# A fused attention and feed-forward block: features scaled in place of weights, four query tiles finished early, and the projection's rest in row-split runs

## The chip, the cores and the metric

The kernel runs on one core of a Trainium2 chip, as one program. The metric is the device time of one execution in microseconds (us). The engines are TensorE (PE; its weight loads are PEld), VectorE (DVE), ScalarE (ACT), GpSimd (POOL) and SyncE (SP). Each works through its own queue in order, and semaphores tie the queues together. SP does nothing but issue transfers; a transfer that waits for its data holds up those issued behind it.

## What is computed

One transformer block on x, 2048 tokens (S) by 576 features (D), with 32 heads of 18 and a hidden layer of 4608, all in bf16:

```
sa, ca, ga, sb, cb, gb = silu(c) @ w_mod          # six rows of 576
h  = layernorm(x) * (1 + ca) + sa
q, k, v = h @ wqkv                                # 32 heads of 18
phi(y) = [softmax(y @ w_phi), softmax(-y @ w_phi)]
o  = (phi(q) @ (phi(k).T @ v)) / (phi(q) @ sum(phi(k)) + 1e-6)
x  = x + ga * (o @ wo)
h  = layernorm(x) * (1 + cb) + sb
x  = x + gb * (relu(h @ w1) @ w2)
```

## The kernel before

The tokens are 16 tiles of 128. The work has a head, which an order written out by hand sets, and then eight blocks of the feed-forward, two tiles each.

**The head.** ORDER is a string of words; a loop (L671) calls a job for each, so every engine gets its instructions in that order. A number after a colon is the pair of PSUM banks that the job writes. The jobs:
- `sc`, `sh` (L251): the two modulation rows of the first norm, with matmuls on zeros between (`Z` are such matmuls alone, L235). `ca` (L509) makes ca1 = 1 + ca, one value per feature and so one per partition.
- `FK` (L442) and `FQ` (L259): w_phi folded into the weights of k and q, in five chunks of 116 features. Each chunk leaves PSUM twice: scaled by ca1 into wk or wq (`fs` L451, `fsd` L448, `fsr` L623, `FQs` L636) and unscaled into wfold (`fra`, `frd` L455 and L457, `frr` L625, `FQra`, `FQrd` L515 and L517). `wsd` (L524) scales the five chunks of the weights of v.
- `KR`, `VR` (L268), `KRh` (L482), `KRd` (L486): four constant rows from the unscaled weights, put into the fifth chunk at rows 96 to 99. `QR`, `QRh`, `QRe`, `QRd` do it for q, by four small transfers.
- `bn` (L240, L241), `sa` (L588 to L590), `sp` (L594 to L596): mean and deviation of each token; `T`, `Tc` (L582, L585) turn them into rows 96 to 99 of the turned features xT. Mean and shift thus come out of the matmul, and 1/deviation is the exponential's scale.
- `K`, `V`, `Q` (L274): the projections, ten matmuls for each tile; `Ka` and `Kb` are four chunks and the fifth. `eK`, `eQ` (L279): both exponentials. `sK` (L284) row sums, `rK` (L301, L302), `pA` (L599), `pM` (L603, L604, L291), `vE` (L305): the softmax factors; `kv` (L324) adds a tile to phi(k).T v in banks 6 and 7, from five buffers E_sb and four buffers v_sb.
- `sq`, `qi` (L336, L339): a query tile of exponentials goes to DRAM and back, since EQ holds six tiles (SLOT); tiles under QF = 2 stay on chip. `qs` (L284, L343), `qp` (L346, L291), `qt` (L350): their factors and the turned tile in ET, of four places.
- `m2`, `ga`, `gb`, `gaw`, `gar`: the other modulation rows; `wo` (L642) multiplies wo by ga on POOL. `wl`, `w2a`, `w2b`: the loads of w1 and w2 into the places of the earlier weights and of xT. `tp` (L479): differences of blocks of w2.
- `kz`, `nu` (L391), `nO` (L398, L399), `ot`, `oc`, `W` (L408, L410), `lb`, `lr`, `ap`, `xc`, `ht`, `hd`, `ha`: tiles 0 and 1 go through the rest of the attention and the second norm. `W` adds x by a matmul with an identity (L408).

**The blocks.** Block b takes tiles 2b and 2b + 1 through the feed-forward: the first layer in three groups (L688, and L695, whose 64-row halves run side by side), relu (L702 to L704), and the second layer (L748) by seven products of half size in 14 positions, with sums on DVE and POOL (L724, L756, L760, L733 to L735). Hooks put the attention of the next two tiles between: `q_next` (qs, qp, qt and a qi three tiles on), `attend` (nu, nO and a transpose by transfer, L403), the projection with wo, residual and norm (L415, L240, L418, L424, L403), and the scaling of h (L872), for which the next block waits. Blocks 0 and 1 do the projection whole in the second layer (wo_mm, L410); blocks 2 to 6 do the rest of 64 rows right behind L695 (wo_rest, L815) and the other 512 rows in the next step (wo_full, L821). Block 7 has no next tiles.

Of the kernel before, what the change touches and what calls it, by code (L numbers as in the profile page):

```python
# [982 lines left out]
```

## Time and profile before

| | |
|---|---|
| median of 5 runs (lowest to highest) | 391.55 us (390.61 to 391.59) |
| the profiled execution | 391.45 us |
| its span on the core | 389.7 us |
| TensorE clock granted | 1.00 |
| head: to the first matmul of block 0 | 93.38 us |
| block 7 begins | 351.65 us |
| DMA | 44.36 MB, mean 114 GB/s |
| sq and qi: transfers of 288 KB | 14 and 14 |

The span is the time between the first and the last instruction that the profile records; the execution's time is longer by 1.75 us. A row of the profile has the line of the kernel, the engine, the operation, what it writes and reads, a count, the busy time, and the mean duration of one in ns. Matmuls are pipelined: one of 288 columns is listed with 286 ns, but thirty in a row take 3.68 us. "Idle before" is the time that the engine stood still just before an instruction, with the instruction that ended it.

### The profile page before, as it was taken

The page shows a single profiled execution, that of the slowest core. Times are in us where ns is not written, and L with a number is a line of the kernel's source. Part 1 is how long each engine was busy: PE and PEld are TensorE (multiplying, and loading weights), DVE is VectorE, ACT ScalarE, POOL GpSimd, SP SyncE. Part 2 cuts the span into 40 slices and gives each one's busy share as a digit, 9 for nine tenths or more (in the row PEclk, how much of TensorE's full clock was granted, in tenths as well). Part 3 has the DMA queues.
Part 4 walks back from the last instruction along what each step waited for, and adds up shares of the span by engine and source line. Part 5 has one row for each costly group of instructions (what it writes and reads, how often), then busy time and mean ns, then how long its engine had stood idle before and what let it go on. Part 6 is the DMA issues. An engine that isn't in the chain of part 4 may idle for free.

```text
span 389.7 us, 8936 instructions
## 1 busy us (share of the span) xinstructions
PE 381.5 (98%) x3710; PEld 310.4 (80%) x3711; DVE 245.0 (63%) x462; ACT 157.7 (40%) x370; POOL 119.6 (31%) x193
## 2 busy tenths in 40 slices
PE   8999999999999999999999999999999999999995
PEld 4777888878887888778878788888888788788884
DVE  1989988954879748755674485468365735542333
ACT  2788779689531233123302430341144114302510
POOL 2164958731101511730061026004500440041023
PEclk9999999999999999999999999999999999999999
DMA  8999839686621252341124124300520223100000
GB/s 300 421 420 398 309 121 358 163 306 211 136 56 35 45 122 52 66 96 30 35 63 108 35 19 90 97 19 19 122 36 19 47 62 35 36 0 32 3 0 32
DMA packets 49515, 44.36 MB, mean 114 GB/s; under 512 B 39361, under 2 KB 42050, under 8 KB 48706
## 3 DMA queue, kind: packets, MB, share of 16 engines
q1 hardware_dynamic: 49186, 43.59, 38.2%
q8 instruction: 29, 0.48, 0.5%
q10 hardware_dynamic: 288, 0.19, 0.2%
q14 instruction: 12, 0.10, 0.1%
HBM read 27.97 MB, written 6.49 MB: 88 GB/s over the span
## 4 chain that ended last, share of the span: by engine, by line
PE 92%; DVE 3%; ACT 2%; DMA 1%; issue 1%; POOL 1%; POOLq 0%; SPq 0%; DVEq 0%; ACTq 0%
PE PS L688 33%; PE PS L748 30%; PE PS L274 14%; PE PS L695 5%; PE PS L821 3%; PE PS L410 2%; PE PS L391 2%; PE PS L324 1%; DMA R<-in_wsc_dram 1%; ACT RT L279 1%; DVE st L240 1%; PE PS L251 1%; DVE h L872 1%; PE PS L442 0%; POOL x_sb L735 0%
## 5 line engine op out<-in xcount | busy, mean ns | idle before, releaser
L688 PE MATMUL PS<-h,R 128*128 128x256 bf16 x1152 | 132.8, 273 | 0.3 <-DVE h L872 0.3
L688 PEld LDWEIGHTS <-R 128*128 128x128 bf16 x1152 | 110.9, 98 | 15.7 <-issue 2.5
L748 PEld LDWEIGHTS <-RH 128*128 128x128 f16 x846 | 82.8, 98 | 20.8
L734 POOL TENSOR_TENSOR yt<-yt,gb_row 128x288 f32<-128x288 f32 x23 | 23.0, 1002 | 192.1 <-DVE yt L733 192.1
L702 ACT ACTIVATE RH<-PS 128x256 f16<-128x256 f32 x72 | 27.5, 382 | 113.4 <-PE PS L695 98.4
L748 PE MATMUL PS<-R,RH 128*128 128x288 bf16 (+1 forms) x558 | 72.4, 286 | 0.0
L704 DVE SCALAR_TENSOR_TENSOR RH<-PS,RH 128x256 f16<-128x256 f32 x72 | 28.9, 413 | 65.6 <-ACT RH L702 65.6
L279 ACT ACTIVATE RT<-PS,rs 128x576 bf16<-128x576 f32 x64 | 42.9, 749 | 8.5 <-PE PS L274 8.3
L703 ACT ACTIVATE RH<-PS 128x512 f16<-128x512 f32 x72 | 42.9, 596 | 6.2 <-PE PS L688 5.2
L748 PE MATMUL PS<-RT,RH 128*128 128x288 f16 x288 | 37.9, 286 | 0.0
L752 ACT ACTIVATE RS<-PS 128x288 f32<-128x288 f32 x24 | 9.8, 410 | 67.8 <-PE PS L748 67.8
L274 PE MATMUL PS<-RH,R 116*128 116x288 bf16 x240 | 31.8, 286 | 0.5 <-ACT RH L636 0.5
L274 PE MATMUL PS<-RH,RT 116*128 116x288 bf16 x240 | 31.7, 286 | 0.0
L274 PEld LDWEIGHTS <-R 116*128 116x128 bf16 x240 | 22.9, 98 | 6.4 <-issue 0.7
L274 PEld LDWEIGHTS <-RT 116*128 116x128 bf16 x240 | 22.7, 98 | 5.5
L733 DVE TENSOR_TENSOR yt<-PS,RS 128x288 f32<-128x288 f32 x23 | 10.4, 452 | 26.2 <-PE PS L748 19.2
L240 DVE BATCH_NORM_STATS2 st<-x_sb 128x6 f32<-128x288 bf16 x60 | 24.2, 445 | 0.5
L735 POOL TENSOR_TENSOR x_sb<-yt,x_sb 128x288 bf16<-128x288 f32 x31 | 22.5, 730 | 2.4 <-DVE yt L731 0.6
L284 DVE TENSOR_REDUCE Rk<-RT 128x64 f32<-128x1152 bf16 x16 | 21.2, 1332 | 1.4 <-ACT RT L279 1.4
L284 DVE TENSOR_REDUCE Rq<-RT 128x64 f32<-128x1152 bf16 x16 | 21.5, 1343 | 0.0
L695 PE MATMUL PS<-h,R 64*128 64x256 bf16 x288 | 19.9, 271 | 0.0
L291 POOL TENSOR_TENSOR RT<-RT,ratq 128x576 bf16<-128x576 bf16 x16 | 19.0, 1190 | 1.3
(125 smaller groups left out, 418.7 us busy)
## 6 DMA issues: line engine op xcount, KB each, us to landing
R<-in_w1a_dram SPq DMA_DIRECT2D x4, 1152.0 KB
eqd<-RT SPq DMA_DIRECT2D x14, 288.0 KB, 4.5
RT<-eqd SPq DMA_DIRECT2D x14, 288.0 KB, 3.0
R<-in_w2a_dram SPq DMA_DIRECT2D x3, 864.0 KB, 10.2
R<-in_w2b_dram SPq DMA_DIRECT2D x2, 1296.0 KB, 10.9
out_dram<-x_sb SPq DMA_DIRECT2D x15, 144.0 KB, 1.7
RT<-in_xT_dram SPq DMA_DIRECT2D x2, 640.0 KB
x_sb<-in_xk_dram SPq DMA_DIRECT2D x3, 288.0 KB
```

Source lines behind the costliest of these rows:

```text
L240: dve.bn_stats(out=s[:, hf, :], in_=x_sb[:, t, hf * HD:(hf + 1) * HD])
L274: pe.matmul(pr[:, k, 0:HD], lhsT=xt(t, ck), rhs=w[0:R, ck, k * HD:(k + 1) * HD], start=(ck == 0), stop=(ck == NC - 1))
L279: act.activation(out=E.rearrange("p (b h s e) -> p b h s e", b=2, s=2, e=DH)[:, :, :, s, :], in_=pr[:, :, 0:HD].rearrange("p b (h e) -> p ...
L284: dve.tensor_reduce(out=Rr, in_=E.rearrange("p (c e) -> p c e", e=DH), axis=AXX, op=ALU.add)
L688: pe.matmul(PS[:, 2 * u + hf, n * 256:n * 256 + 256], lhsT=w1a[:, ci, jj * P:(jj + 1) * P], rhs=hb[:, ci, :], start=(n == 0 and ci == 0), ...
L695: pe.matmul(PS[:, 2 * u + hf, n * 256:n * 256 + 256], lhsT=w1b[b0:b0 + 64, j * P:(j + 1) * P], rhs=hb[b0:b0 + 64, 4, :], start=False, stop ...
L702: act.activation(out=A11[:, j, :], in_=lo[:, :, 0, :], func=ACT.Relu)
L703: act.activation(out=A2[:, j, :, :], in_=PS[:, 2 * u + 1, :].rearrange("p (n s f) -> p n s f", n=2, s=2), func=ACT.Relu)
L704: dve.scalar_tensor_tensor(out=U3[:, j, :], in0=lo[:, :, 1, :], scalar=0.0, in1=A11[:, j, :], op0=ALU.max, op1=ALU.subtract)
L734: pool.tensor_tensor(out=y, in0=y, in1=gb_row[:, c], op=ALU.mult)
L735: pool.tensor_tensor(out=x_sb[:, t, c], in0=y, in1=x_sb[:, t, c], op=ALU.add)
L748: pe.matmul(PS[:, bank, 0:HD], lhsT=am[:, j, :], rhs=bm[:, j, :], start=first and j == 0, stop=(j % 9 == 8), skip_group_check=True)
```

## The change

- xT is multiplied by ca1 in place, two tiles at a time (x_scale): tiles 0 to 3 on DVE (`xd`), 6, 10 and 14 with their neighbours on POOL (`xp`), 4, 8 and 12 on ACT (`xa`). The weights of k, q and v stay unscaled: wfold, wv_raw and their copies go.
- The constant rows of k and v are made in halves of 288 columns.
- QF = 4: tiles 2 and 3 stay on chip and are turned in the head. Their trips to DRAM go.
- The identity matmul of `W` goes, and `xr` adds x on DVE, as in the blocks.
- Blocks 0 and 1 do the projection's rest as the later blocks do, with hooks at other places; a new one, "first", stands behind the first run of a group.
- One subtraction of block 1 goes from POOL to DVE.
- The first loads come in another order, and ORDER is written anew.

The core of the diff:

```diff
--- before.py
+++ after.py
@@ -41,21 +41,21 @@


 ORDER = """
-Z11 sx sd rp sc FK ca Z2 fs0 fsr frr fra2 sh frd4 fra0 fra1 bn1 fs3 bn0 fs1 Z1 fra3 shc sa0 wsd2 KR:0 fsd4 fs2
-sp0 bn2 T0:2 VR:1 KRh bn3 Tc0 Ka0:2 KRd sa2 wsd1 sp2 VRh Kb0 wsd0 Ka1:0 wsd4 eKa0 VRd Kb1 wsd3 T2:1 eKa1 sK0
-V0:2 Tc2 sK1 FQ3:0 rK0 K3:1 FQra3 pA0 FQs3 pM0 vE0 eK3 K2:0 bn4 bn5 rK1 kv0 eK2 FQ1:2 pA1 V1:1 sK3 pM1 FQra1
-m2:0 vE1 rK3 sa4 pA3 sK2 FQs1 kv1 sp4 V2:1 m2c pM3 bn7 rK2 T4:2 V3:0 bn6 Tc4 pA2 vE2 pM2 sa6 K4:2 vE3 K5:1
-bn10 eK4 sp6 bn9 T6:0 kv2 Tc6 kv3 eK5 sK4 ga:2 K7:0 gac sK5 rK4 K6:1 eK7 pA4 pM4 bn8 V4:2 eK6 sK7 gb:0 sa8
-V5:1 vE4 wl0 rK7 sp8 rK5 sK6 pA7 T8:2 gbc kv4 pA5 Tc8 FQ2:0 pM5 K8:2 vE5 rK6 FQrd2 K9:1 bn11 eK8 w2a2 pA6 pM6
-bn14 kv5 sa10 V6:2 FQs2 sK8 eK9 sp10 wl1 V7:0 pM7 vE6 rK8 sK9 T10:1 V8:2 Tc10 pA8 vE7 pM8 K10:1 rK9 vE8 w2a0
-kv6 bn12 eK10 FQ0:0 pA9 FQ4:2 kv7 pM9 FQrd0 kv8 FQrd4 V9:1 FQs0 w2b0 bn13 FQs4 QR:0 vE9 K11:2 QRh sa12 QRe
-sK10 sp12 kv9 eK11 V10:1 bn15 QRd wl4 rK10 T12:0 V11:2 sK11 Tc12 pA10 sa14 pM10 K13:0 gbw vE10 rK11 wl2 Q0:1
-pA11 eK13 sp14 vE11 pM11 kv10 eQ0 T14:2 sK13 K12:0 w2a1 Tc14 qs0 kv11 rK13 K14:1 eK12 pA13 pM13 V13:2 eK14
-sK12 wl3 K15:0 qp0 vE13 rK12 sK14 V12:1 eK15 pA12 pM12 qt0 Q1:2 vE12 rK14 sK15 gbr V14:0 pA14 eQ1 gaw pM14
-kv12 vE14 rK15 kv13 V15:1 qs1 pA15 gar pM15 kv14 Q2:2 vE15 qp1 kv15 eQ2 Q3:0 tp0 wo4 qt1 kz Q4:1 eQ3 wo2 sq2
-tp2 Q5:2 eQ4 sq3 tp1 wo3 nu0:3 eQ5 Q6:0 sq4 nO0 wo0 qi2 Q7:1 eQ6 wo1 sq5 ot0:2 w2b1 eQ7 nu1:3 Q8:0 nO1 oc0
-Q9:1 eQ8 W0:3 eQ9 sq7 lb0 ot1:2 sq8 Q10:0 oc1 sq6 lr0 W1:1 ap0 eQ10 sq9 lb1 xc0 ht0:2 sq10 Q11:0 ha0 hd0 lr1
-Q12:3 eQ11 ap1 Q13:2 qi3 xc1 eQ12 sq11 ht1:0 Q14:1 hd1 ha1 sq12 eQ13 Q15:3 qi4 eQ14 sq13 eQ15 sq14 sq15
+sx sd bn0 Z11 sc FK bn1 sa0 ca sh frd4 fra1 fra2 frr xd0 bn2 shc bn3 sp0 T0:2 fra3 fra0 Ka0:0 Tc0 xd2 KR:2
+KRh0 KRd0 KRh1 KRd1 sa2 VR:1 sp2 Z1 Kb0 VRh0 VRd0 Ka1:2 VRh1 VRd1 rp eKa0 T2:1 Tc2 bn5 Kb1 eKa1 sK0 FQ2:0
+FQrd2 K2:1 K3:2 FQ4:0 sK1 xp6 eK2 V1:1 FQrd4 V0:0 bn4 rK0 pA0 rK1 pA1 vE1 eK3 m2:2 pM0 vE0 FQ3:0 sa4 xa4 sK2
+m2c FQra3 bn6 sp4 V2:1 pM1 rK2 pA2 pM2 bn7 T4:2 kv0 kv1 Tc4 vE2 FQ1:0 bn8 FQra1 K4:2 sa6 FQ0:1 FQrd0 K5:0 sp6
+T6:1 xp10 eK4 kv2 Tc6 sK3 eK5 QR:2 K7:1 rK3 pA3 pM3 sK4 V3:0 QRh eK7 QRe QRd K6:2 rK4 pA4 bn9 vE3 sK5 sa8 eK6
+ga:1 gac bn13 kv3 sp8 V4:0 V5:1 vE4 pM4 kv4 sK6 rK5 pA5 T8:0 vE5 gaw xa8 Tc8 pM5 gar w2b0 xp14 wo2 Q0:2 rK6
+pA6 pM6 eQ0 bn10 gb:0 gbc gbw kv5 Q1:1 K9:0 bn11 sa10 sK7 sp10 qs0 qp0 eQ1 eK9 rK7 pA7 sK9 K8:2 eK8 Q2:1 eQ2
+V6:0 rK9 pM7 wl0 wl4 sK8 vE6 Q3:2 eQ3 bn12 V7:1 rK8 pA8 vE7 pM8 kv6 qs1 w2a0 T10:0 sa12 sp12 V8:2 bn14 Tc10
+vE8 w2a2 pA9 xa12 qp1 bn15 kv7 K10:0 eK10 wl1 K11:1 eK11 qt0 sK10 kv8 wl3 T12:2 Tc12 pM9 V9:0 vE9 rK10 V10:1
+sK11 wl2 pA10 sa14 sp14 kv9 rK11 K12:0 eK12 w2a1 pM10 pA11 pM11 vE10 K13:2 qs2 sK12 kv10 T14:1 eK13 V11:0 vE11
+rK12 Q4:2 sK13 kv11 wo0 Tc14 V12:1 K14:0 pA12 vE12 K15:1 rK13 qs3 pM12 kv12 qp2 eQ4 qt1 eK14 sK14 sq4 gbr pA13
+pM13 V13:2 vE13 eK15 Q5:0 sK15 kv13 rK14 pA14 V14:2 pM14 rK15 pA15 pM15 qt2 V15:1 vE14 kv14 Q6:2 qp3 vE15 kv15
+eQ5 sq5 Q7:1 kz tp0 eQ6 eQ7 wo1 Q8:0 nu1:3 nO1 eQ8 nu0:1 nO0 sq6 tp1 Q9:2 ot1:3 oc1 sq7 Q10:0 tp2 qt3 ot0:3
+oc0 wo3 wo4 W1:1 xr1 lb1 sq8 Q11:3 eQ10 W0:1 xr0 w2b1 eQ9 lb0 eQ11 sq11 Q12:2 lr1 Q13:1 eQ12 sq9 qi5 qi4 lr0
+eQ13 ap1 ap0 Q14:3 sq13 ht1:2 ht0:0 ha1 hd1 ha0 hd0 Q15:1 sq10 sq12 eQ15 sq15 qi6 eQ14 sq14
 """

 @with_exitstack
...
-    QF = 2
+    QF = 4
     RE = small([P, NET * 9 * P], BF16, "RE")
     ET = carve(RE, 0, (NET, 9, P))
...
-    wv_raw = carve(R1, 12760, (NC, D))
-    wfold = carve(R1, 15640, (NC, D))
...
     load(sp, flat(wsc), "wsc")
+    load_x(0, 2)
     load(sp, flat(wkT), "wkT")
+    load(sp, flat(wsh), "wsh")
     load_xT(0)
-    load(sp, flat(wsh), "wsh")
-    load_x(0, 2)
-    load(sp, flat(wv_raw), "wv")
     load_x(2, 2)
     load_xT(1)
-    load_x(4, 2)
+    load(sp, flat(wv), "wv")
     load(sp, epsr[:], "epsr")
     load(sp, flat(wqT), "wqT")
+    load_x(4, 2)
     load_xT(2)
...
-    def wo_mm(t, pr, add_x=False):
+    def wo_mm(t, pr):
         for k in range(2):
-            if add_x:
-                pe.matmul(pr[:, k, 0:HD], lhsT=ident[:, 0:P], rhs=x_sb[:, t, k * HD:(k + 1) * HD], start=True, stop=False)
             for ci in range(NC):
                 pe.matmul(pr[:, k, 0:HD], lhsT=oT[:, t % 2, ci, :], rhs=wo_sb[:, ci, k * HD:(k + 1) * HD],
-                          start=(ci == 0 and not add_x), stop=(ci == NC - 1))
+                          start=(ci == 0), stop=(ci == NC - 1))

...
-        if src is None:
-            cols(xn[:, t % 2, 0:D], x_sb[:, t, :])
-            cols(xn[:, t % 2, D:640], x_sb[:, t, 512:D])
-        else:
-            cols(v2(xn[:, t % 2, 0:D]), src[:, :, 0:HD])
-            cols(xn[:, t % 2, D:640], src[:, 1, 224:HD])
+        cols(xn[:, t % 2, 0:D], x_sb[:, t, :])
+        cols(xn[:, t % 2, D:640], x_sb[:, t, 512:D])
...
-    def f_scaled(dst, ck):
-        act.activation(out=dst[0:R, ck, 0:G5], in_=PS[0:R, ck, 0:G5], func=ACT.Copy, scale=ca1[0:R, ck:ck + 1])
-
     def f_raw(eng, ck):
         if eng is act:
-            act.activation(out=wfold[0:R, ck, 0:G5], in_=PS[0:R, ck, 0:G5], func=ACT.Copy)
+            act.activation(out=wk[0:R, ck, 0:G5], in_=PS[0:R, ck, 0:G5], func=ACT.Copy)
         else:
-            eng.tensor_copy(out=wfold[0:R, ck, 0:G5], in_=PS[0:R, ck, 0:G5])
+            eng.tensor_copy(out=wk[0:R, ck, 0:G5], in_=PS[0:R, ck, 0:G5])
...
-    def rows_h(pr):
-        act.activation(out=v2(tmpr[X0:NX, :]), in_=pr[X0:NX, :, 0:HD], func=ACT.Copy)
-
-    def rows_d(pr, dst):
-
-        dve.scalar_tensor_tensor(out=v2(dst[X0:NX, 4, :]), in0=v2(tmpr[X0:NX, :]), scalar=mk[X0:NX, :],
-                                 in1=pr[X0:NX, :, 0:HD], op0=ALU.mult, op1=ALU.add)
+    def rows_h(pr, k):
+        c = slice(k * HD, (k + 1) * HD)
+        act.activation(out=tmpr[X0:NX, c], in_=pr[X0:NX, k, 0:HD], func=ACT.Copy)
+
+    def rows_d(pr, dst, k):
+
+        c = slice(k * HD, (k + 1) * HD)
+        dve.scalar_tensor_tensor(out=dst[X0:NX, 4, c], in0=tmpr[X0:NX, c], scalar=mk[X0:NX, :],
+                                 in1=pr[X0:NX, k, 0:HD], op0=ALU.mult, op1=ALU.add)
...
+
+    def x_scale(t, eng):
+
+        xT, o, nt, j = XOFF[t]
+        if eng is pool:
+            v = xT[0:R, o:o + NC * nt * P].rearrange("p (c f) -> p c f", c=NC)[:, :, j * P:(j + 2) * P]
+            pool.tensor_tensor(out=v, in0=v, in1=ca1[0:R, :].unsqueeze(2).to_broadcast([R, NC, 2 * P]), op=ALU.mult)
+            return
+        for ck in range(NC):
+            v, f = xt(t, ck, 2), ca1[0:R, ck:ck + 1]
+            if eng is act:
+                act.activation(out=v, in_=v, func=ACT.Copy, scale=f)
+            else:
+                dve.tensor_scalar(out=v, in0=v, scalar1=f, scalar2=None, op0=ALU.mult)
...
-    def wv_scale(ck, eng):
-        o, i, f = wv[0:R, ck, :], wv_raw[0:R, ck, :], ca1[0:R, ck:ck + 1]
-        if eng is act:
-            act.activation(out=o, in_=i, func=ACT.Copy, scale=f)
-        else:
-            eng.tensor_scalar(out=o, in0=i, scalar1=f, scalar2=None, op0=ALU.mult)
...
-    def ln2_bn(i, pr):
-        for hf in range(2):
-            dve.bn_stats(out=st[:, i, hf, :], in_=pr[:, hf, 0:HD])
-        dve.bn_aggr(out=mv[:, 1, i, :], in_=st[:, i])
...
-    ROWS = {"K": wfold, "V": wv_raw, "Q": wfold}
-    ROWD = {"K": wk, "V": wv, "Q": wq}
+    ROWS = {"K": wk, "V": wv, "Q": wq}
...
-        "fs": lambda c: f_scaled(wk, c), "fsd": lambda c: f_scaled_d(wk, c),
         "frd": lambda c: f_raw(dve, c), "fra": lambda c: f_raw(act, c),
-        "fsr": lambda: dve.tensor_tensor(out=wk[0:R, :, G5:D], in0=last,
-                                         in1=ca1[0:R, :].unsqueeze(2).to_broadcast([R, NC, FW]), op=ALU.mult),
-        "frr": lambda: dve.tensor_copy(out=wfold[0:R, :, G5:D], in_=last),
+        "frr": lambda: dve.tensor_copy(out=wk[0:R, :, G5:D], in_=last),
...
-        "wsd": lambda c: wv_scale(c, dve), "wsa": lambda c: wv_scale(c, act), "wsp": lambda c: wv_scale(c, pool),
+        "xd": lambda t: x_scale(t, dve), "xp": lambda t: x_scale(t, pool), "xa": lambda t: x_scale(t, act),
...
-        "FQs": lambda c: act.activation(out=v2(wq[0:R, c, :]), in_=at["FQ", c][0:R, :, 0:HD], func=ACT.Copy, scale=ca1[0:R, c:c + 1]),
-        "FQrd": lambda c: raw_copy(dve, v2(wfold[0:R, c, :]), at["FQ", c][0:R, :, 0:HD]),
-        "FQra": lambda c: raw_copy(act, v2(wfold[0:R, c, :]), at["FQ", c][0:R, :, 0:HD]),
+        "FQrd": lambda c: raw_copy(dve, v2(wq[0:R, c, :]), at["FQ", c][0:R, :, 0:HD]),
+        "FQra": lambda c: raw_copy(act, v2(wq[0:R, c, :]), at["FQ", c][0:R, :, 0:HD]),
...
-        "W": lambda i: wo_mm(i, at["W", i], True), "lb": lambda i: ln2_bn(i, at["W", i]), "lr": ln2_rs,
-        "xc": lambda i: act.activation(out=v2(x_sb[:, i, :]), in_=at["W", i][:, :, 0:HD], func=ACT.Copy),
-        "ap": lambda i: ln2_apply(i, at["W", i]),
...
+        "W": lambda i: wo_mm(i, at["W", i]), "xr": lambda i: add_res(i, at["W", i]), "lb": lambda i: bn(1, i), "lr": ln2_rs,
+        "ap": lambda i: ln2_apply(i),
...
-        JOBS[w + "Rh"] = lambda w=w: rows_h(at[w + "R", None])
-        JOBS[w + "Rd"] = lambda w=w: rows_d(at[w + "R", None], ROWD[w])
+        for k in range(2):
+            JOBS[f"{w}Rh{k}"] = lambda w=w, k=k: rows_h(at[w + "R", None], k)
+            JOBS[f"{w}Rd{k}"] = lambda w=w, k=k: rows_d(at[w + "R", None], ROWS[w], k)
...
                 l1_full(js[u], u, range(cut[u]), hb)
+                if u == 0:
+                    hooks(g, "first")
...
-            (pool if b == 1 else dve).tensor_tensor(out=A12, in0=A12, in1=U2, op=ALU.subtract)
+            dve.tensor_tensor(out=A12, in0=A12, in1=U2, op=ALU.subtract)
...
-        if t > 5:
+        if t > 1:
...
         def in_l1(g, u):
             if not more:
                 return
-            if b < 2:
-                if (g, u) in ((0, -1), (0, 1)):
-                    q_next(t0 + max(u, 0))
-                if (g, u) in ((1, 2), (2, 1)):
-                    attend(t0 + g - 1)
-                if b and (g, u) == (2, 2):
-                    q_next(t0 + 2)
-                return
-            if (g, u) in ((0, 0), (0, 2)):
-                attend(t0 + u // 2)
+            if (g, u) in (((0, 0), (1, "first")) if b == 1 else ((0, 0), (0, 2))):
+                attend(t0 + int(u in (2, "first")))
+            if b == 0 and (g, u) == (1, "first"):
+                q_next(t0 + 2)
             if g and u == "rest":
                 wo_rest(t0 + g - 1, pair(3))
             if g and u == 0:
...
         def in_l2(pos):
             if not more:
                 return
-            if b < 2 and pos in (1, 4):
-                i = pos // 4
-                wo_mm(t0 + i, pair(i))
-                add_res(t0 + i, pair(i))
-                bn(1, t0 + i)
-            if b < 2 and pos == 2:
-                norm2(b, t0)
-            if pos == (6 if b < 2 else 1):
+            if pos == 1:
                 norm2(b, t0 + 1)
-            if pos == (12 if b < 2 else 8):
+            if pos == (8 if b else 12):
                 hb = h2[:, (b + 1) % 2]
                 for ci in range(NC):
                     dve.tensor_scalar(out=hb[:, ci, :], in0=hb[:, ci, :], scalar1=mod2[:, 1, ci:ci + 1],
                                       scalar2=mod2[:, 0, ci:ci + 1], op0=ALU.mult, op1=ALU.add)
-            if b > 1 and pos in (4, 10) or b == 1 and pos == 8:
-                q_next(t0 + 2 + pos // 8)
+            if pos in ((4, 10) if b else (12,)):
+                q_next(t0 + 2 + int(pos > 4))
...
```

## The prediction

> **What bounds the kernel now.** I read the page first, the chain of waits next, then the table of windows by stage, then TensorE's own timeline.
>
> ```profile
> PE 381.5 (98%) x3710; PEld 310.4 (80%) x3711; DVE 245.0 (63%) x462; ACT 157.7 (40%) x370; POOL 119.6 (31%) x193
> ...
> PE 92%; DVE 3%; ACT 2%; DMA 1%; issue 1%; POOL 1%; POOLq 0%; SPq 0%; DVEq 0%; ACTq 0%
> ```
>
> TensorE is 92% of the chain that ended last, and the page's clock row is 9 in all 40 slices. So an edit counts only through fewer matmul passes, or through shorter waits of TensorE. The other engines count where TensorE waits for them. By stage (columns: length, then PE, PEld, DVE, ACT, POOL busy, clock, DMA share, GB/s):
>
> ```profile
> 10.00:20.00 10.00, 9.20 (x85) 7.44 (x85) 9.66 (x25) 7.96 (x19) 1.26 (x6) 1.00 1.02 418
> 20.00:30.00 10.00, 9.51 (x135) 7.61 (x133) 8.92 (x17) 8.37 (x24) 7.17 (x19) 1.00 1.02 419
> ...
> 40.00:50.00 10.00, 10.00 (x121) 8.51 (x119) 9.85 (x19) 7.28 (x19) 9.24 (x21) 1.00 0.87 338
> ...
> 60.00:70.00 10.00, 10.00 (x109) 8.23 (x107) 8.87 (x10) 7.51 (x17) 8.53 (x18) 1.00 0.95 315
> 70.00:80.00 10.00, 9.14 (x99) 7.33 (x97) 8.23 (x10) 8.37 (x13) 8.23 (x7) 1.00 0.72 204
> ```
>
> In the head (to 93.4 us, where block 0 starts) DVE is nearly as full as TensorE, and ACT and POOL are not far behind. The two places where TensorE stood still after the first matmuls, and the blocks of the feed-forward, from the same table with other edges:
>
> ```profile
> 22.42 1.39 PE L274 MATMUL PS<-RH,R 116*128 116x288 bf16 x10 [0.49 <-ACT RH L636]
> ...
> 78.96 0.45 PE L534 MATMUL PS<-ident,o_sb 128*128 128x128 bf16 x5 [0.86 <-ACT RT L279]
> ```
> ```profile
> 93.38:130.43 37.05, 37.05 (x349) 30.39 (x347) 28.39 (x49) 13.24 (x29) 6.44 (x9) 1.00 0.36 88
> 130.43:167.99 37.56, 37.27 (x350) 30.41 (x348) 25.90 (x47) 10.61 (x25) 15.78 (x16) 1.00 0.37 80
> ...
> 204.79:241.51 36.72, 36.72 (x349) 30.18 (x347) 21.59 (x43) 10.56 (x27) 8.96 (x12) 1.00 0.30 59
> ```
>
> Blocks 0 and 1, which use the whole projection in the second layer, are longer than a later block by 0.33 and 0.84 us.
>
> **The blocks.** Blocks 0 and 1 now take the form of blocks 2 to 6. Per query tile 10 passes (L410, 1.23 us) become two half-row matmuls side by side (L815, 0.12 us, behind the L695 run) and 8 passes (L821, 1.08 us), with fewer changes of row form: two tiles are the 0.33. In block 1 the scaling of h (L872) moves from position 12 to 8, which takes away the wait at 167.6 (some 0.45 us of the 0.84). In block 0 it stays at 12, where block 0 before had no wait. The attends (nu) of block 0 move to where later blocks have them. In block 1 the second comes behind the first run of group 1 and must clear bank pair 3 before the row-split rest: 1.3 + 0.76 us of matmuls lie between, against 0.36 + 0.76 us of DVE (L398, L399), so 0.8 us is spare. q_next(4) adds 1.34 + 0.35 us to DVE in group 1 of block 0, some 9 us of DVE in 8.5 us; the banks are wanted over 1 us after DVE's late reads, so I cost it at nothing (0.8 us if it misses). q_next(5), at position 12, is attended 2.2 + 8.2 = 10.4 us later in block 1; scaling of h, row sums, POOL's step and transpose (issue, landing) take 2.1 + 1.7 + 1.4 + 1.3 + 3.2 = 9.7 us, so 0.7 us is spare. L760 goes from POOL (4.55 us) to DVE (1.35 us) in block 1, as it is in the later blocks. **Sum: -1.17 us**, bounds 0 to -1.3.
>
> **The head: passes.** From the end of "sh" (12.3 us) I count what TensorE still has to do in the new order: 480 projection matmuls and 20 each for the constant rows and for wo (30 in 3.68 us: 0.1227 each), 63.8; kv 16 x 0.345 and its epsilon 0.43, 5.9; five fold chunks 1.65; second modulation 1.23; three quarter jobs 1.3; transposes 0.9 + 1.12; nu 0.75; one spin 0.22. That is 76.9 us, and the four identity matmuls (L408, 0.12 each, -0.49) are gone. Without any wait block 0 starts at 89.2. Before, it started at 93.38 for 77.4 us of passes: 3.7 us were waits, 0.95 of them at 78 (o_sb late, DVE held by t_part), the rest between 12.3 and 24.2.
>
> **The head: does TensorE wait less?** Removed ahead of the first K: scaled copies of the fold on ACT (L451, 4 x 0.69) and DVE (L448 0.74, L623 0.53), and five L524 (0.36 each); later, five L636 on ACT (0.73 each). Added: the scaling of the features in place. No row shows it. On DVE (10 instructions, 116x256 bf16) the nearest is L872 (0.25 to 1.33, median 0.34): I take 0.2 pitch, 1 us for a pair of tiles. On ACT (15) L702 and L585 (0.38): 0.3 to 0.38, 1.5 to 1.9 a pair. On POOL (3, 1280 elements) L291 gives 2.0 ns an element (1.17 us for 576): 2.5 us each, 7.6 in all. So ACT's and DVE's sums hardly change; what changes is that less lies ahead of K0.
>
> Loads: wsc landed at 5.76, wsh at 10.15, with 1770 KB between: 403 KB per us. By that rate x0 and x1 (288 KB, moved ahead) land at 6.5 and fill DVE's idle time with two bn jobs; wkT lands at 8.3 and holds up the fold by 0.4 us, which ends at 9.8; wsh at 10.1 as before; xT0 at 10.9, wv at 14.1. Raw copies end at 11.3 on ACT, the scaled features at 11.9, and Ka0 can follow sh at 12.4. The half-width constant rows (288 columns: about half of L482's 0.64 and L486's 0.82) let Kb0 start at 16.1 where TensorE arrives anyway; before, the first exponential came at 17.46, behind L486 and L482. Stepping on by the same durations, TensorE finds each operand 0 to 0.7 us early up to 29 us, and is then ahead of before by one K (1.23) and two fold chunks (0.66).
>
> Queues that moved steps pass: SP loses four 288 KB transfers (sq2, sq3, qi2, qi3) and gets two transposes (qt2, qt3, 1.25 to 2.1 us of issue each). On POOL wo2 now waits for the broadcast of ga_row with pA6 and pM6 queued behind it; store and broadcast took 6.5 us before (67.1 to 73.6), and 7.1 us of POOL work lie ahead of it. qs2 and qs3 (1.69 us of DVE each) come from block 0. The residual add is back (L415, 0.75 x2) and normalising reads SBUF (0.63 for a tile, was 1.13).
>
> Deadlines, with block 0 at 89.2: the eight last Q with nu, turns and wo take 14.1, so Q8 starts at 75.1 and the last kv at 73.5. DVE's list from the first row sum to the last L305 was 48.4 us busy; with qs2 and qs3 51.8, from 16.9: it may idle 4.8 us, and idled 3.6. POOL's list was 38.5 us busy and 12.2 idle between 21.2 and 71.9; with the three scalings, qp2 and two wo it is 50.1 us from 18.3: it may idle 5.1. POOL is the tight one. The end: hd0 is ready 1.8 us after the turns' start, the passes there take 1.5. **I put 1.2 us of waits on all this (an estimate: some 0.4 each for the first steps with no spare time, the two full lists and the end): the head gives -4.2 + 1.2 = -3.0 us**, bounds -4.2 and +2.9 (rival C).
>
> *A rule weighed.* The tp rows ran 1.05 to 1.14 us alone and 2.08 and 2.13 beside POOL's L642, which itself went from 1.28 to 2.09. The Trainium skill, "SBUF — State Buffer", section "Who interferes with whom", says that a DVE instruction with two SBUF inputs, or in a two-port mode, and a POOL instruction that reads SBUF exclude each other, and that one with a single SBUF input outside those modes does not contend. The rows agree. By the rule the new POOL scalings block none of the row sums, statistics or L305 they run beside, and cost DVE nothing; if each blocked DVE for its length, it would be 7.6 us.
>
> **Sum.** Execution before: 391.45 us (span 389.7); the median of the runs is 0.10 above it. 391.45 - 3.0 - 1.17 = 387.3, and with that 0.1, **387.4 us**.
>
> **Rivals.**
> *A. The head isn't shortened.* Copies only change place, ACT and DVE are as full as before, and TensorE still starts late. What stays is 0.49 + 0.95 + 1.17: 388.9 (388.3 to 389.5). For it: DVE at 9.66 of 10 in 10 to 20 us. Against: eleven copies fewer ahead of K0.
> *B. A transfer at the end of the head.* w2b1 (1296 KB, 10.9 us to landing before) is now issued within 10 us of block 0, ahead of sq9; eQ9 waits for qt3, eQ15 for sq9, and block 0's second bank pair for eQ15. sq9 issues some 4.5 us before block 0 and the eqd transfers took 2.4 to 7.4 us to land; eQ15 wants it at once: 0 to 2.5 us more, 387.4 to 389.9. For it: 16 DMA engines at 0.9 to 1.0 in 78 to 86 us. Against: four transfers fewer.
> *C. POOL becomes the bound (slower).* In-order POOL keeps the idle time of before, because its scalings wait for xT and its row steps for ACT: 12.2 where 5.1 may be, kv is 7.1 us late, E_sb's five buffers fill, and K and V stop. Time: 391.45 - 4.2 - 1.2 + 7.1 = 393.2. It decides the sign from about 10.5 us of idle (5.4 beyond what may be). For it: 9.24 of 10 at 40 to 50 us. Against: half of the idle time was POOL waiting for work, which the scalings fill.
>
> **How the numbers follow.** My case (386.1 to 388.3) 0.50; A 0.17; B beyond that 0.12; C and the like 0.21, of which 0.08 within 0.2% (0.8 us, about what a measurement of this kernel can tell from no change) and 0.13 slower. Faster: 0.50 + 0.17 + 0.12 = 0.79. The range runs from no wait at all (386.1) over A and B into the lower part of C: 386.0 to 391.8 leaves some 0.17 out, most of it above.
>
> **What would show it.** Block 0 should start near 90.4 (89.2 to 93); blocks 0 and 1 should last 36.7 to 37.0; no L534 wait of 0.9; K0's exponential near 16.5; POOL idle under 6 us from 18 to 74. Wrong if TensorE's waits for L305, L291 or the feature scalings sum to over 2 us in 16 to 75, if eQ15 stands behind sq9, or if L872 ends late in block 0.

## The result and the profile after

The changed kernel's median is 389.88 us (389.42 to 391.89), that of the kernel before 391.13 us in runs beside it: a ratio of 0.9978 with a 95% interval of 0.997 to 0.9986. It became faster, by less than a third of what was forecast. The ratio is nearer to 1 than the two medians because 13 of 36 executions had a granted clock of 0.996 and took 391.1 to 391.9 us; the last three runs below look for the reason.

The profiled execution took 389.63 us, with a span of 387.9 and a clock of 1.0. First the page's busy times and its chain of waits:

```profile
PE 380.6 (98%) x3703; PEld 310.5 (80%) x3705; DVE 242.6 (63%) x470; ACT 156.8 (40%) x380; POOL 125.3 (32%) x195
...
PE 90%; ACT 5%; DVE 2%; DMA 1%; issue 1%; POOL 1%; POOLq 0%; DVEq 0%; ACTq 0%
```

TensorE still holds the chain, with 0.9 us less work. Then the stages of the head and the first blocks in the table of windows (length, then PE, PEld, DVE, ACT, POOL busy, clock, DMA share, GB/s):

```profile
10.00:20.00 10.00, 9.63 (x96) 8.13 (x96) 8.85 (x27) 7.12 (x17) 1.38 (x5) 1.00 1.03 421
20.00:30.00 10.00, 9.96 (x142) 8.16 (x141) 9.82 (x20) 8.51 (x27) 8.30 (x17) 1.00 1.02 417
...
70.00:80.00 10.00, 10.00 (x116) 8.36 (x114) 7.38 (x10) 6.26 (x12) 8.98 (x13) 1.00 0.64 159
```
```profile
91.54:128.32 36.78, 36.78 (x348) 30.23 (x347) 28.10 (x50) 13.32 (x31) 9.01 (x7) 1.00 0.36 89
128.32:166.83 38.51, 36.88 (x348) 30.17 (x347) 23.27 (x46) 10.56 (x27) 10.24 (x13) 1.00 0.32 49
166.83:203.55 36.72, 36.72 (x349) 30.20 (x347) 21.59 (x43) 10.56 (x27) 8.95 (x12) 1.00 0.30 68
```

In the three slices of the head TensorE gained 0.43, 0.45 and 0.86 us of busy time. The surprise is block 1: 38.51 us long with only 36.88 us of matmuls. What changed, stage by stage (us):

| | before | after | measured | forecast |
|---|---|---|---|---|
| block 0 begins | 93.38 | 91.54 | -1.84 | -3.0 |
| block 0 lasts | 37.05 | 36.78 | -0.27 | -0.33 |
| block 1 lasts | 37.56 | 38.51 | +0.95 | -0.84 |
| block 2 lasts | 36.80 | 36.72 | -0.08 | 0 |

The sum is -1.24, which is also the medians' difference. The last transfer is issued 1.25 us earlier (385.42, was 386.67); the span shrank by 0.55 us more because the last transfer was followed by 2.5 us, where it was 3.0.

TensorE's timeline has two waits behind the modulation:

```profile
18.28 0.47 PE L257 MATMUL PS<-RS,R 126*116 126x126 bf16 x6 [0.26 <-ACT RT L277]
```
```profile
140.62 0.30 PE L802 MATMUL PS<-wo_sb,oT 64*128 64x288 bf16 x2 [1.63 <-DMA oT<-o_sb]
```

The waits of 0.49 at 22 us and 0.86 at 79 us are gone. The new one, in block 1, is for the transposed output of tile 4. That tile, o_sb, was complete at 134.1 us, so the transposing transfer had 4.9 us until TensorE wanted it at 139.0. SP's own timeline (the start of each issue and how long SP was at it) shows why that was not enough:

```profile
127.53 0.34 SPq L765 DMA_DIRECT2D out_dram<-x_sb  x1
131.61 1.29 SPq L348 DMA_TRANSPOSE RE<-RT  x1
136.25 0.33 SPq L337 DMA_DIRECT2D RT<-eqd  x1
136.68 0.39 SPq L769 DMA_DIRECT2D out_dram<-x_sb  x1
137.15 2.63 SPq L401 DMA_TRANSPOSE oT<-o_sb  x2
```

q_next(5), now at position 12, issues two transfers: it turns tile 5 (L348) and then fetches tile 8 (L337) into the very buffer that the first one reads. So the fetch stands at the head of SP's queue until the turn has landed, from 132.9 to 136.25. Behind it stand an output store and the transpose that TensorE waits for. (The same line, L337, waits for a turn nine times in this kernel, 21.2 us in all; among TensorE's listed waits only this one shows.) The chain of waits says the same:

```profile
136.54 0.39 PE PS L389 x10
...
137.15 3.42 DMA oT<-o_sb
...
140.62 0.30 PE PS L802 x2
```

### The profile page after: what moved, and what is told of

Read it like the earlier page. It is cut to its first block, busy times and chain, and to the rows that moved or that the text cites. A ratio compares the mean times of both kernels' runs of the same rounds, so it can differ in the third digit from the quotient of the medians.

```text
span 387.9 us, 8925 instructions
## 1 busy us (share of the span) xinstructions
PE 380.6 (98%) x3703; PEld 310.5 (80%) x3705; DVE 242.6 (63%) x470; ACT 156.8 (40%) x380; POOL 125.3 (32%) x195
## 4 chain that ended last, share of the span: by engine, by line
PE 90%; ACT 5%; DVE 2%; DMA 1%; issue 1%; POOL 1%; POOLq 0%; DVEq 0%; ACTq 0%
PE PS L673 32%; PE PS L735 31%; PE PS L272 11%; PE PS L680 5%; PE PS L808 4%; ACT RT L277 3%; PE PS L233 2%; PE PS L389 2%; PE PS L322 1%; PE PS L249 1%; DMA oT<-o_sb 1%; PE PS L406 1%; PE PS L802 0%; PE PS L257 0%; ACT RT L511 0%
## 5 line engine op out<-in xcount | busy, mean ns | idle before, releaser
L721 POOL TENSOR_TENSOR yt<-yt,gb_row 128x288 f32<-128x288 f32 x23 | 28.0, 1219 | 204.5 <-DVE yt L720 204.5
L272 PE MATMUL PS<-RH,R 116*128 116x288 bf16 x240 | 32.5, 286 | 0.1
L272 PE MATMUL PS<-RH,RT 116*128 116x288 bf16 x240 | 31.9, 286 | 0.3
L238 DVE BATCH_NORM_STATS2 st<-x_sb 128x6 f32<-128x288 bf16 x64 | 25.9, 446 | 4.0 <-DMA x_sb<-in_xk_dram 3.5
L272 PEld LDWEIGHTS <-RT 116*128 116x128 bf16 x240 | 22.9, 98 | 6.0 <-issue 0.5
L272 PEld LDWEIGHTS <-R 116*128 116x128 bf16 x240 | 22.7, 98 | 5.9 <-issue 0.4
L282 DVE TENSOR_REDUCE Rk<-RT 128x64 f32<-128x1152 bf16 x16 | 21.3, 1336 | 0.9 <-ACT RT L277 0.7
L282 DVE TENSOR_REDUCE Rq<-RT 128x64 f32<-128x1152 bf16 x16 | 21.5, 1343 | 0.0
L411 DVE TENSOR_TENSOR x_sb<-x_sb,PS 128x576 bf16<-128x576 bf16 x16 | 12.0, 753 | 13.2 <-PE PS L808 12.1
```

The source lines that it names most:

```text
L238: dve.bn_stats(out=s[:, hf, :], in_=x_sb[:, t, hf * HD:(hf + 1) * HD])
L272: pe.matmul(pr[:, k, 0:HD], lhsT=xt(t, ck), rhs=w[0:R, ck, k * HD:(k + 1) * HD], start=(ck == 0), stop=(ck == NC - 1))
L282: dve.tensor_reduce(out=Rr, in_=E.rearrange("p (c e) -> p c e", e=DH), axis=AXX, op=ALU.add)
L721: pool.tensor_tensor(out=y, in0=y, in1=gb_row[:, c], op=ALU.mult)
```

## The experiments

Each line number below is of the kernel in question; in those whose ORDER was edited the string stands in one line, and the numbers behind it are 14 lower than in the kernel after (L258 is its L272).

**1. The fetch of tile 8 issued later.** Theory S: the fetch in SP's queue is the whole of block 1's loss. Rival T: the transpose is late for another reason.

```diff
-    def q_next(q):
+    def q_next(q, load=True):
...
-            if q + NL < NT:
+            if q + NL < NT and load:
...
                 attend(t0 + int(u in (2, "first")))
+                if b == 1 and u == 0:
+                    q_in(8)
...
-                q_next(t0 + 2 + int(pos > 4))
+                q_next(t0 + 2 + int(pos > 4), b > 0)
```

> One transfer moves on SP: the load of tile 8's exponentials (q_in, which overwrites the buffer that tile 5's transpose reads) is issued behind the transpose of oT for tile 4 instead of ahead of it. Theory S (SP's queue: q_in waits until tile 5's transpose has landed, and the oT transpose stands behind it): block 1 falls from 38.51 us to 36.7 to 36.8, no wait of TensorE for oT, time 1.7 to 1.8 us below the changed kernel, some 388.1, 0.992 of before. Rival T (the transpose itself takes 3.4 us there, or o_sb is late): block 1 stays above 38 us and the time within 0.3 us of the changed kernel's 389.9.

It took 387.75 us (387.65 to 387.92), a ratio of 0.9908 [0.9894, 0.9922] to the kernel before. Block 1 and SP's queue:

```profile
128.14:165.05 36.91, 36.89 (x348) 30.12 (x347) 23.30 (x46) 10.58 (x27) 10.24 (x13) 1.00 0.35 51
```
```profile
131.43 1.29 SPq L348 DMA_TRANSPOSE RE<-RT  x1
132.93 0.41 SPq L769 DMA_DIRECT2D out_dram<-x_sb  x1
133.94 1.59 SPq L401 DMA_TRANSPOSE oT<-o_sb  x1
136.36 0.33 SPq L337 DMA_DIRECT2D RT<-eqd  x1
```

With the fetch behind it, the transpose is issued at 133.94, as soon as its data is there, and block 1 loses its wait. Theory S holds, T falls. The 0.19 us that block 1 is still longer than block 2 is for the most part a wait of the second attend (136.39) for tile 5's turned factors: the 0.7 us that the prediction called spare do not exist.

**2. The whole projection in blocks 0 and 1 again.** The row-split runs undone, with the hooks of before around them.

```diff
-            if (g, u) in (((0, 0), (1, "first")) if b == 1 else ((0, 0), (0, 2))):
-                attend(t0 + int(u in (2, "first")))
+            if b < 2:
+                if (g, u) in ((1, 2), (2, 1)):
+                    attend(t0 + g - 1)
+                return
...
+            if b < 2 and pos in (1, 4):
+                i = pos // 4
+                wo_mm(t0 + i, pair(i))
...
-            if pos == (8 if b else 12):
+            if pos == (12 if b < 2 else 8):
```

> Blocks 0 and 1 do the projection whole in the second layer again, with the attends late in groups 1 and 2; the new head, tiles 2 and 3 finished there, and the new places of q_next stay. Theory S: the oT transposes are wanted so late that the SP wait is hidden: block 0 goes back to 37.05 us, block 1 to 37.1 to 37.6, so 0.7 to 1.1 us faster than the changed kernel: about 389.0. The row-split form is then worth 0.3 us for block 0 and costs 0.9 to 1.4 in block 1 as it stands. Rival (the wait comes from the new place of q_next, not from the early attends): block 1 stays near 38.5 and block 0 gains nothing: 390.2.

It took 394.47 us, 1.0076 [1.0061, 1.0091], far from what I expected. Block 0, measured from its first matmul to that of block 1, is 37.05 (91.18 to 128.23), as long as in the kernel before (93.22 to 130.27). In the kernel after it is 36.71 by the same edges (91.44 to 128.15). So the row-split form is worth 0.34 there, as forecast (0.33); the 0.27 of the table comes from other edges. Block 1 is another matter:

```profile
160.17 1.27 SPq L348 DMA_TRANSPOSE RE<-RT  x1
165.08 0.33 SPq L337 DMA_DIRECT2D RT<-eqd  x1
165.47 1.21 SPq L401 DMA_TRANSPOSE h<-xn  x1
```
```profile
169.35 5.27 PE L673 MATMUL PS<-h,R 128*128 128x256 bf16 x28 [3.91 <-DVE h L857]
```

With my hooks the same pair, turn and fetch, came ahead of the transpose of h, and TensorE waited 3.91 us. That is theory S at a second place. The 28 matmuls behind the wait also took 5.27 us; elsewhere they take 3.22. I come back to that.

**3. No scaling of the features.** Two experiments price the scaling by leaving it out. In this one the kernel after loses its eight `x` jobs; the factor 1 + ca of the first norm is left out of the computation.

```diff
-KRh0 KRd0 KRh1 ... xd0 ... xd2 ... xp6 ... xa4 ... xp10 ... xa8 ... xp14 ... xa12
+KRh0 KRd0 KRh1 ...
```

> The changed kernel without its eight scalings of the features; it leaves out the factor 1 + ca, the rest is the same. Theory H (TensorE waits 2.1 us in the new head; the scalings cause the 0.33 us at 55.8, where ACT's scaling took 2.1 us, and little of the 0.85 us between 16 and 24): block 0 starts 0.3 to 0.7 us sooner than 91.5. Rival (the scalings fill DVE, ACT and POOL and set the head): 1.5 to 2 us sooner, near 89.6.

It took 389.92 us, 0.997 [0.9958, 0.9981]; block 0 begins at 90.85 to 90.95, 0.6 us earlier, and the small wait at 56 us is gone. Of the 0.6, 0.14 is there already when the modulation ends (12.35 for 12.49 us), 0.15 more comes by 24 us and 0.3 at 56 us. Against experiment 1, which has the scalings, block 0 begins 0.4 earlier (90.85 for 91.27). So the scalings cost 0.4 to 0.6 us of the head. The whole time, 389.92, is that of the kernel after within the intervals; the wait for oT in block 1 is still there, with 1.72 us.

**4. The kernel before without the scaling of its weights.** The scaled copies `fs`, `fsd`, `fsr`, `FQs` and `wsd` go, and the raw copies feed the projections; again 1 + ca is left out.

```diff
-    load(sp, flat(wv_raw), "wv")
+    load(sp, flat(wv), "wv")
...
-            act.activation(out=wfold[0:R, ck, 0:G5], in_=PS[0:R, ck, 0:G5], func=ACT.Copy)
+            act.activation(out=wk[0:R, ck, 0:G5], in_=PS[0:R, ck, 0:G5], func=ACT.Copy)
```

> The kernel before without its scaled copies (four on ACT and two on DVE for k, five on DVE for v, five on ACT for q); raw copies go where the scaled ones went, so it leaves out the factor 1 + ca; order of all else as before. It is what scaling the weights cost. Theory H: TensorE's 2.1 us of waits between 12 and 24 us come from these copies and shrink to about 0.7; block 0 starts at 91.8 to 92.3 instead of 93.4 and the time falls by 1.1 to 1.6 us. Rival A (the copies only filled time in which TensorE waited for the modulation row and the constant rows): block 0 starts within 0.4 us of 93.4.

It took 390.17 us, 0.9967 [0.9953, 0.998]; block 0 begins 1.1 us earlier (first matmul at 92.13 for 93.22). But not all of this is the price of the copies. TensorE is 0.4 us ahead of the kernel before at 24 us, and still 0.4 at 75 us (the first nu starts at 74.70 for 75.10). Then the wait at 79 us vanishes here as well, which brings the lead to 1.4, and 0.35 is lost again before block 0. In this execution the modulation ended 0.7 us later than in the kernel before; counted from its end, the lead gained by 24 us is 1.1. So the copies cost 0.4 to 1.1 us where they stand, the scaled features 0.4 to 0.6, and turning one into the other is worth somewhere between nothing and 0.7 us.

The wait at 79 us hangs on something smaller. In the kernel before, a pair of differences on DVE starts just behind POOL's products of wo and takes 4.17 us, and o_sb is late by it:

```profile
73.67 4.17 DVE L479 TENSOR_TENSOR RT<-R 128x1728 f16<-128x1728 bf16 x2
```
```profile
73.60 7.84 POOL L642 TENSOR_TENSOR wo_sb<-wo_sb,ga_row 128x576 bf16<-128x576 bf16 x5 [1.69 <-DMA ga_row<-gatd]
```

In this experiment the same pair starts at 73.26, ahead of POOL's products (73.80), and takes 3.09 us. So a lead of 0.4 us became one of 1.4.

**5. q_next(5) two positions earlier.** Another way to get the turn out of the way of the transpose.

```diff
-            if pos in ((4, 10) if b else (12,)):
+            if pos in ((4, 10) if b else (10,)):
```

> The changed kernel with tile 5's q_next moved from position 12 of block 0 to position 10, as in the later blocks; nothing else. SP then has the transpose, and the load that overwrites its buffer, behind it before the oT transpose of block 1 is ready. Theory S: block 1 lasts 36.72 us, 1.8 less, and the time is 0.1 to 0.3 us below the kernel with the load moved alone (0.9908 of before), since tile 5's turned factors are no longer late for the second attend either (0.13 us there). Rival: DVE's row sums at position 10 hold up the scaling of h, and block 1 starts 0.3 to 1 us later, which eats that up.

388.36 us, 0.9931 [0.992, 0.9943]. Block 1 is 37.28 us, without the wait for oT, but its first 28 matmuls take 3.79 us instead of 3.22. They use h, and DVE and POOL show why it is late:

```profile
124.53 1.34 DVE L282 TENSOR_REDUCE Rq<-RT 128x64 f32<-128x1152 bf16 x1
...
126.72 2.68 DVE L846 TENSOR_SCALAR h<-h,mod 128x256 bf16<-128x256 bf16 x5
```
```profile
126.70 1.17 POOL L289 TENSOR_TENSOR RT<-RT,ratq 128x576 bf16<-128x576 bf16 x1
```

The row sums now stand ahead of the scaling of h, but do not delay its start: it begins 1.57 us before block 1's first matmul in both kernels (126.40 and 127.97 in experiment 1). It takes 2.68 us instead of 1.78. POOL's multiplication, which follows the row sums, now runs beside it, where in experiment 1 it came at 130.24. Moving the fetch is better than moving the whole step, by 0.37 us of block 1. The rest of the difference to experiment 1 lies in the head, which is the same in both: block 0 begins 0.3 us later here (91.59 for 91.27). So much it varies between executions on different chips.

**6. Tiles 12 and 13 scaled on DVE.** From here on all edits are made to the kernel of experiment 1, to see what the head's waits consist of. `xa12` becomes `xd12`.

```diff
-vE8 w2a2 pA9 xa12 qp1 bn15 kv7
+vE8 w2a2 pA9 xd12 qp1 bn15 kv7
```

> On top of the kernel with the load moved: the features of tiles 12 and 13 are scaled on DVE (five instructions, 1.06 us for a pair) instead of ACT (2.1 us). Theory H: ACT is the chain behind TensorE's wait at 55.8 us, so that wait (0.33 us) goes and block 0 starts 0.3 us sooner than 91.36; time 387.4, 0.990 of before. Rival: DVE is as full there (9.7 of 10 in 50 to 60 us), and the wait stays or moves: no change from 387.75.

390.56 us (389.16 to 391.85), 0.999 [0.9975, 1.0006]: 2.8 us worse than experiment 1, and block 0 begins at 95.10 in the profiled execution. I had missed two things. The five instructions took three times their estimate:

```profile
54.61 2.90 DVE L499 TENSOR_SCALAR RT<-RT,ca 116x256 bf16<-116x256 bf16 x5
...
59.61 0.75 DVE L289 TENSOR_TENSOR RT<-PS,Ak 128x576 bf16<-128x576 f32 x1
```

The ten of this form at 11 to 15 us, with POOL idle or nearly so, took 0.23 to 0.28 us each; of these five one took 1.20. POOL ran two of its 1.17 us multiplications (L275) from 54.56 to 55.73 and from 56.22 to 57.43. The Trainium skill, "SBUF — State Buffer", section "Who interferes with whom", says that a DVE instruction in a two-port mode and a GpSimd instruction exclude each other for the whole length of one; this run agrees, with 2.90 us for work that takes 1.06 alone. TensorE, which waits for the L289 behind it, then lost twice:

```profile
60.42 0.51 PE L308 MATMUL PS<-RT 128*128 128x76 bf16 x9 [2.38 <-DVE RT L289]
60.76 4.29 PE L258 MATMUL PS<-RH,RT 116*128 116x288 bf16 x20
```

It waited 2.38 us, and the next 20 matmuls took 4.29 us instead of 2.62. The windows name the reason (the number behind POOL's is the granted clock):

```profile
58.00:60.40 2.40, 0.03 (x1) 0.00 (x0) 2.37 (x5) 0.64 (x3) 0.03 (x1) 1.00 0.74 201
60.40:62.00 1.60, 1.58 (x17) 1.26 (x17) 1.60 (x2) 0.62 (x4) 1.44 (x7) 0.79 0.85 340
62.00:63.50 1.50, 1.50 (x8) 0.94 (x7) 1.50 (x2) 0.92 (x3) 1.50 (x4) 0.50 1.16 485
63.50:65.00 1.50, 1.50 (x12) 0.98 (x10) 1.15 (x3) 0.72 (x2) 1.42 (x4) 0.58 0.95 399
```

Behind the wait the clock fell to a half for over 3 us. The same explains the 5.27 us in experiment 2, where the windows show 0.50 from 171.0 to 172.5 us.

**7. The identity matmuls back.** Four of them on zeros, one per bank of `W`.

```diff
+            pe.matmul(pr[:, k, 0:HD], lhsT=ident[:, 0:P], rhs=zero[:, 0:HD], start=True, stop=False)
...
-                          start=(ci == 0), stop=(ci == NC - 1))
+                          start=False, stop=(ci == NC - 1))
```

> On top of the kernel with the load moved: the four matmuls with the identity are put back into the head's projections, on zeros instead of x, so that the result stays the same. Theory: the head's end is TensorE's own time there, so they cost their 0.49 us in full: block 0 starts 0.4 to 0.5 us later, time 388.2. Rival: the end of the head waits for the second norm anyway (0.3 us before the last projection), and they cost 0.2 us or less.

388.30 us, 0.993 [0.9917, 0.9943]: 0.55 us above experiment 1. Experiment 5, which ran beside it, has the same head without them and reaches the first `W` within 0.02 us of it (82.09 and 82.07); block 0 begins 0.47 later here (92.06 for 91.59). TensorE is the bound at that place, and a pass removed there counts in full.

**8. One difference ahead of the output step.** In the kernel before, `tp1` stood ahead of `nO`; the new order puts it behind. Here it is put back.

```diff
-wo1 Q8:0 nu1:3 nO1 eQ8 nu0:1 nO0 sq6 tp1 Q9:2
+wo1 Q8:0 nu1:3 tp1 nO1 eQ8 nu0:1 nO0 sq6 Q9:2
```

> On top of the kernel with the load moved: the second of the head's three differences of w2 (tp) is put ahead of the first tile's output step on DVE, as the order before had it. Theory: this is the wait of 0.95 us that the kernel before had at 78 us, and it comes back: the difference takes 1.05 us alone and 2.1 beside POOL's wo, 0.25 us were spare, so block 0 starts 0.8 to 1.9 us later, time 388.5 to 389.6. Rival: TensorE's wait there was for the exponentials on ACT, as the profile's releaser said, and nothing changes (within 0.3 us of 387.75).

389.12 us, 0.9954 [0.9942, 0.9966]: 1.4 us above experiment 1, and the wait is back where it was:

```profile
81.29 0.45 PE L510 MATMUL PS<-ident,o_sb 128*128 128x128 bf16 x5 [1.22 <-DVE o_sb L383]
```

So the order of two words in DVE's list was worth more than the change that the kernel is named after (0 to 0.7 us, experiments 3 and 4).

**9. Tiles 12 and 13 scaled on POOL.** The question of rival C: was POOL tight?

```diff
-gaw xa8 Tc8 pM5 gar w2b0 xp14 wo2
+gaw xa8 Tc8 pM5 gar w2b0 xp14 xp12 wo2
...
-vE8 w2a2 pA9 xa12 qp1
+vE8 w2a2 pA9 qp1
```

> The version with the load moved behind the second attend, but tiles 12 and 13 are scaled on POOL (one instruction, L506) right behind tiles 14 and 15, ahead of wo2, and no longer on ACT at 53 us. This asks whether POOL was as tight as rival C had it. Theory of slack: POOL idled 9.65 us of 57 in the head and TensorE's buffers take up a delay of one or two us, so 2.3 us more on POOL cost TensorE nothing; the 2.1 us less on ACT take the wait at 55.8 away (0.2 to 0.33). Block 0 starts 0.1 to 0.4 earlier (91.0 to 91.3), 387.4 to 387.7. Theory of a tight POOL (rival C): behind the wait for ga_row POOL's list has no free time until 51 us, so its row steps come 1.2 to 2.3 us late, kv stands, and block 0 starts 0.5 to 2 us later: 388.3 to 389.8. The scaling itself should take 2.3 us, as the other three.

387.85 us, 0.9917 [0.9904, 0.9931], the same as experiment 1 within the intervals. POOL was busy for 49.57 of the 57 us from 18 to 75, idle for 7.43 where it had 9.46 in experiment 1, and block 0 begins at 91.48, within the spread of this head (91.27 in experiment 1, 91.59 in experiment 5). The two scalings took 4.60 us together. A tight POOL is refuted. The 0.3 us that TensorE lost at 55.8 went, as forecast, but 0.17 before 52.5 and 0.23 before 58.5 came in their place, so nothing was gained.

**10 to 12. The changed kernel three times more.** Experiments 2 and 6 had shown a half clock behind a long wait. The changed kernel has a wait of 1.63 us in block 1; does that explain its executions at 0.996? Nothing was edited.

> The changed kernel once more, for its clock. Of its 36 timed executions 13 had a granted clock of 0.996 and took 391.1 to 391.9 us, the others 0.998 to 1.0 and 389.4 to 390.3. Theory G: the 1.63 us for which TensorE stands still in block 1 (oT of tile 4) sometimes lowers the clock behind it; an execution with 0.996 then shows a clock near 0.5 in the 3 to 4 us after 140.6 us, the same 38.5 us of block 1 plus some 1.7, and full clock elsewhere. Rival: the lower clock has nothing to do with the wait, and lies at another place or is spread over the whole span. An execution with 1.0 (some two in three) tells nothing, but must show block 1 at 38.5 and no slice below 1.0 behind the wait.

> As the run before it: with a mean clock of 0.996, theory G expects about 0.5 in the 3 to 4 us behind the wait for oT of tile 4 in block 1 and block 1 near 40.2 us; the rival expects the low clock elsewhere. With 1.0, block 1 at 38.5.

> As the two runs before it: with a mean clock of 0.996, about 0.5 in the 3 to 4 us behind the wait in block 1 (theory G) or elsewhere (rival); with 1.0, block 1 at 38.5 us.

The three took 391.56, 391.34 and 389.85 us, with clocks of 0.996, 0.996 and 1.0. TensorE waited for oT for 1.89, 1.99 and 1.85 us. The windows of the first, around the wait:

```profile
137.00:140.50 3.50, 1.90 (x23) 1.27 (x20) 1.40 (x3) 1.13 (x3) 0.00 (x0) 1.00 0.98 210
140.50:142.00 1.50, 1.22 (x8) 0.76 (x9) 0.00 (x0) 0.00 (x0) 0.00 (x0) 0.77 0.13 24
142.00:144.00 2.00, 2.00 (x11) 1.32 (x10) 1.06 (x2) 0.25 (x1) 0.00 (x0) 0.50 0.00 0
144.00:146.00 2.00, 2.00 (x17) 1.64 (x16) 1.19 (x5) 1.12 (x3) 0.00 (x0) 0.82 0.00 0
```

The second shows 0.79, 0.50 and 0.80 in the last three of these windows, the third 1.00 throughout. On the pages of the first two the clock row has its only dip in the slice of these windows. From first matmul to first matmul, block 1 lasts 40.44, 40.55 and 38.74 us. Theory G holds: the wait costs its own length and, in some executions, 1.7 to 1.8 us more through the clock.

## Why the prediction was wrong, and where it was right

The forecast was 387.4 us, with -4.17 us for the change; -1.24 came by the stages. The miss of 2.9 us has two parts.

**Block 1, 1.79 us: the step that failed is "q_next(5), at position 12, is attended 2.2 + 8.2 = 10.4 us later in block 1; ... so 0.7 us is spare".** I followed q_next(5) down to the attend that needs it, and counted its turn, but not its second transfer, the fetch of tile 8 that q_next also issues. That fetch waits for the turn's source to come free, holds SP's in-order queue for 3.4 us, and the transpose of tile 4's output, which I had not listed as queued behind it, comes 3 us late. It was a plain omission: the prediction counted SP's issues for the head, not for the blocks. Shown by experiment 1, which takes the fetch alone out of the way and gains 1.60 us of block 1, and a second time by experiment 2. The 0.7 us of spare time were wrong too: with the queue free, tile 5's factors still land just as they are wanted (0.13 to 0.19 us lost).

**The head, 1.16 us: the mis-sized term is "I put 1.2 us of waits on all this".** "Sh" ended at 12.49 instead of 12.3, and from there to block 0 lie 79.05 us for the 76.9 us of passes: 2.15 us of waits. Counting passes along the timeline, about 1.0 us is lost by 24 us (of which rows show 0.26 for the first exponential, begun at 16.85 where I had put it near 16.5), 0.4 more by 42, some 0.3 near 56, and 0.3 in the last Q before block 0. The windows show only 0.69 us of idle TensorE from 10 us to block 0, so the 2.15 are what the count of passes leaves over, an estimate; they are many small losses. Scaling the features is part of them: 0.4 to 0.6 us by experiment 3. What the edits of the head brought can be added up from the experiments: 0.47 to 0.55 for the identity matmuls, some 0.9 to 1.4 for the wait at 79 us, and of the measured 1.84 some 0.5 or less remains for all else, where the sum had 3.0 - 0.49 - 0.95 = 1.56.

What held:
- *The blocks' form.* -0.33 was forecast for block 0; it is -0.27 by the table's edges and -0.34 from first matmul to first matmul. Block 1 ran 36.91 when its queue was free, for 36.72.
- *The identity matmuls, -0.49.* Experiment 7: 0.47 of the head, 0.55 of the whole time.
- *The wait at 79 us goes* (-0.95 forecast), because o_sb was late behind t_part. Experiment 8 brings 1.2 us of it back with one word; experiment 4 loses it without touching that word, so it hangs on a few tenths of a microsecond.
- *Prices of the scaling.* 1.02 to 1.06 a pair on DVE (1 forecast), 2.32 on POOL (2.5), but 2.1 on ACT, where 1.5 to 1.9 was forecast. The DVE price holds only without POOL beside it (experiment 6).
- *POOL's scalings cost DVE nothing.* The row sums beside them (L282 at 20.97 and 31.15 us, L506 at 19.56 and 30.39) took 1.30 to 1.34 us, as elsewhere.

The rivals: **A** (the head is not shortened, 388.9) came nearer to the measured time than my case, in part by chance, since most of the loss lay in block 1. But in the head it was nearer too: it has 0.49 + 0.95 = 1.44 us there, my case 3.0, and 1.84 was measured. Its view that the copies only change place is off by 0.4 us, mine by 1.16. **B** (eQ15 behind sq9) did not occur; no such wait is in the trace. **C** (POOL the bound) was too strict in its arithmetic. From 18.3 to 73.5 us POOL was busy for 45.95 us where I had counted 50.1, and idled 9.25 where I had allowed 5.1; 2.3 us more of work on it cost nothing that shows (experiment 9).

Experiment 1 at 387.75 us is faster than both kernels, and 0.35 above the forecast.

What stays open: which of the small losses of the head belongs to which edit, and so what scaling features in place of weights is worth by itself; and what decides whether a wait of nearly 2 us lowers the clock.

## What to carry to other kernels

When a step is moved, write down every transfer that it issues, and for each the buffer it overwrites: a fetch into a place that another transfer still reads stands at the head of the queue until that one lands, and what matters is who is queued behind it. Issue such a fetch behind the transfers that TensorE is waiting for. And price a wait of TensorE of some 2 us or more at its length plus the slower matmuls that can follow.
